# A zero-pass filler with a higher target and true job sizes, and a start with its blanking moved between engines, in a gated mix of two attention blocks

## Chip, cores, metric

The kernel runs on one core of one Trainium2 chip. The metric is device time in microseconds (us). The time is about 1.8 us more than the span from the first to the last instruction that the profile shows. A run counts as slow when it is over 1.5% above the fastest of the same kernel; only fast runs enter ratios.

## The reference, cut to what matters

```python
g = sigmoid((x * gate_w).sum(-1))          # x: 2048 x 512, bf16
a = softmax_attention(x, A_wqkv, A_wo)     # 32 heads of 16, all 2048 x 2048 scores
b = local_attention(x, B_wqkv, B_wo)       # 32 heads, 8 keys at distance 0, 2, .. 14
return g * a + (1 - g) * b
```

Block `a` needs 32 x 2048 x 2048 exponentials. They are the bulk of the work.

## The kernel before

The attention of block `a` runs in 32 periods, one for each pair of a 512-row piece of the queries and a group of four heads. In a period TensorE writes scores into two PSUM tiles (`ring`, of 1536 and of 1024 columns), ScalarE takes exponentials of them (`pT`), and TensorE multiplies those with V into the accumulator `acc`. About a tenth of the score tiles goes to a bank `w` and gets its exponential from a polynomial on VectorE (`ta`, `pd`). GpSimd does block `b`.

The order of all instructions is fixed when the kernel is built: a small event simulation, the plan, has queues, durations and priorities, and emits instructions in its own order of time. The plan also fills idle stretches of TensorE with matmuls of a zero weight, "zero passes", so that the clock gate does not halve TensorE's clock:

```python
    HAM = 3.4133                  # us, the length of one step of the clock gate
    share = 0.55                  # target: streamed share of such a step
    def idle_fill(self, st):      # st: when the next TensorE job can start
        t = self.free["pe"]
        gap = st - t - 0.18
        if self.filler is None or gap < 0.1:
            return
        lo = st - self.HAM
        ...
        have = sum(b - max(a, lo) for a, b in self.streamed)
        need = min(gap, self.share * self.HAM - have)
        if need < 0.05:
            return
        d = self.filler(need)
        if d:
            self.stream(t, d)
            self.free["pe"] = t + d
    ...
    # a job of planned duration x[4] counts as x[4] - 0.11 us of streaming:
    self.stream(st, x[4] - 0.11)
```

```python
    def fill_pass(need):
        p = acc_open[0]
        if p is None:                       # before the first accumulator: into a bank of its own
            ...
        j = max(range(4), key=lambda j_: row_left[p][j_])
        if row_left[p][j] == 0:             # accumulator complete: no pass
            return 0.0
        n = int(need * 2400.0 / 64.0) * 64
        done = 0
        while done < n:                     # adds zero to the open accumulator
            m = min(QW, n - done)
            mm(acc_tiles[p][32 * j:32 * j + 32, 0:m], z32[:], filling(m), False, False, tile_position=(0, 32 * j))
            ...
```

A zero pass lies in a planned gap and ends 0.18 us before the next job, so it moves nothing else in the plan.

At the start, the projection weights are spread from `wraw` into padded tiles `wkp` and `wqp`, whose padding must be zero. GpSimd (`G`) blanks most of it; VectorE (`V`) copies the first columns of `wqp`:

```python
    V.memset(wqp[:, :, 0:1], 0.0)
    for i0, i1 in ((0, 1), (1, NG)):
        G.memset(wkp[:, :, i0:i1], 0.0)
        G.tensor_copy(out=wkp[:, :, i0:i1, ...], in_=wraw[:, 0, :, i0 * 64:i1 * 64] ...)
        if i0 == 0:
            G.memset(wqp[:, :, 1:NG], 0.0)
    ...
    def w_job():
        yield ("delay", 8.0)
        yield ("dve", 1, 1.0, lambda: wq_part(V, 0, 1))
        yield ("set", ev_wq)
```

Of the kernel before, what the change touches and what calls it, by code (L numbers as in the profile page):

```python
# [19 lines left out]
DH = 16  # L20
# [31 lines left out]
class Plan:  # L52
# [79 lines left out]
            return  # L132

    HAM = 3.4133
    share = 0.55
    filler = None

    def stream(self, t, d):
        self.streamed.append((t, t + d))

    def idle_fill(self, st):
# [6 lines that stand above are left out]
        while self.streamed and self.streamed[0][1] < lo:  # L148
            self.streamed.popleft()
        have = sum(b - max(a, lo) for a, b in self.streamed)  # L150
        need = min(gap, self.share * self.HAM - have)
        if need < 0.05:
            return
        d = self.filler(need)
        if d:
            self.stream(t, d)
            self.free["pe"] = t + d
# [16 lines left out]
    def run(self):  # L174
        while True:
            best = None
            for e, lst in self.ready.items():
                rs = []
                for x in lst:
                    g_ = self.gate(x[6])  # L180
                    if g_ is not None:
                        rs.append(max(x[2], g_))
                if rs:
                    st = max(self.free[e], min(rs))
                    if best is None or st < best[0]:
                        best = (st, 1, e)
            for r, lst in self.reqs.items():
                if lst and self.slots[r]:
                    st = max(min(x[0] for x in self.slots[r]), min(x[2] for x in lst))
                    if best is None or st <= best[0]:  # L190
                        best = (st, 0, r)
            if best is None:
                return
            st, kind, nm = best
            self.now = st
            if kind == 0:
                lst = self.reqs[nm]
                x = min(y for y in lst if y[2] <= st + 1e-9)
                lst.remove(x)
                s = min(y for y in self.slots[nm] if y[0] <= st + 1e-9)  # L200
                self.slots[nm].remove(s)
                self.advance(x[3], st, s[1])
            else:
                lst = self.ready[nm]
                ok = [y for y in lst if y[2] <= st + 1e-9 and self.gate(y[6]) is not None
                      and self.gate(y[6]) <= st + 1e-9]
                x = min(ok, key=lambda y: (y[0], y[1]))
                if nm == "pe" and not self.fits(x, st):
                    for y in ok:
                        y[2] = max(y[2], st + 0.1)  # L210
                    continue
                lst.remove(x)
                if nm == "pe":
                    self.idle_fill(st)
                if x[6] is not None:
                    slot = self.take(x[6], st)
                    self.held["job"] += 1
                    more = x[5](slot)
                else:
                    more = x[5]()  # L220
                if isinstance(more, float):
                    x[4] += more
                if nm == "pe":
                    self.stream(st, x[4] - 0.11)
                if CFG_DEBUG:
                    LOG.append((st, x[4], nm, getattr(x[3], '__name__', '?'), x[0]))
                self.free[nm] = st + x[4]
                self.advance(x[3], st + x[4] + self.LAT[nm], None)
# [3 lines left out]
def kernel(  # L232
# [95 lines left out]
    SP.dma_start(out=awo[:], in_=A_wo.rearrange("(c p) n -> p c n", p=128))  # L328
    warm = const.tile([128, 1], BF16, name="warm")

    make_identity(nc, ident[:])
    V.memset(z32[:], 0.0)
    V.memset(warm[:], 0.0)
    A.activation(out=warm[:], in_=warm[:], func=ACT.Exp)
    heat = ps.tile([128, QW], FP32, tag="acc", bufs=1, name="heat")
    V.memset(wqp[:, :, 0:1], 0.0)
    for i0, i1 in ((0, 1), (1, NG)):
        G.memset(wkp[:, :, i0:i1], 0.0)
        G.tensor_copy(out=wkp[:, :, i0:i1, :, 0:DH].rearrange("p c i j d -> p c (i j) d"),
                      in_=wraw[:, 0, :, i0 * 64:i1 * 64].rearrange("p c (h d) -> p c h d", d=DH))  # L340
        if i0 == 0:
            G.memset(wqp[:, :, 1:NG], 0.0)
    make_identity(nc, identf[:])
    V.memset(selq[:], 0.0)
    for j in range(4):
        V.memset(selq[32 * j:32 * j + DH, 32 * j + DH:32 * j + DH + 1], 1.0)
# [3 lines left out]
    V.scalar_tensor_tensor(out=kbias[:], in0=qbias[:], scalar=256.0, in1=k16[:], op0=ALU.mult, op1=ALU.add)  # L350
    V.tensor_scalar(out=qbias[:], in0=qbias[:], scalar1=VOFF / 256.0, scalar2=None, op0=ALU.mult)

    def wq_part(eng, i0, i1):
        eng.tensor_copy(out=wqp[:, :, i0:i1, :, 0:DH].rearrange("p c i j d -> p c (i j) d"),
                        in_=wraw[:, 1, :, i0 * 64:i1 * 64].rearrange("p c (h d) -> p c h d", d=DH))
    wq_part(G, 1, NG)
    G.memset(vp_all[:, :, :, DH:DH + 1], 1.0)
    G.memset(maskb[:], 0.0)
    G.affine_select(out=maskb[:], in_=maskb[:], compare_op=ALU.is_ge, fill=NEG,
# [1 line left out]
    zpad = work.tile([128, 2 * D], BF16, name="zpad", tag="kvs", bufs=1)  # L361
    G.memset(zpad[:], 0.0)
    SP.dma_start(out=kv_scr[0:16, :], in_=zpad[0:16, :])


    P = Plan(["pe", "act", "dve", "pool", "sp"])
# [54 lines left out]
    ev_kv = [Event() for _ in range(NT)]  # L421
    ev_kdone = Event()
    ev_wq = Event()
    ev_turned = [Event() for _ in range(NC)]
    ev_final = [Event() for _ in range(NC)]
    k_left = [NG * NC]
# [4 lines left out]
    final_left = [TPC] * NC  # L431

    xts = {}
    ev_xfree = {0: Event(), 1: ev_x[1], 2: Event()}

    def x_job(sc):
        yield ("delay", XARR[sc])
# [8 lines left out]
    def x_half(sc, hf, xt, left):  # L446
        v = xt[:, hf, :].bitcast(BF16).rearrange("p (c t) -> p c t", c=DC)

        def tr():
            for tt in range(2):  # L450
                for c in range(DC):
                    PE.transpose(out=v[:, c, tt * 128:(tt + 1) * 128],
                                 in_=xr[sc // 2][:, sc % 2, 2 * hf + tt, c * 128:(c + 1) * 128], identity=ident[:])
        yield ("pe", 0, 0.70, tr)
        dst = xT[:, :, sc * QW + hf * 256:sc * QW + (hf + 1) * 256]
        if hf == 0:
            yield ("dve", 1, 0.62, lambda: V.tensor_copy(out=dst, in_=v))
        else:
            yield ("act", 0, 1.05, lambda: A.copy(out=dst, in_=v))
        left[0] -= 1  # L460
        if left[0] == 0:
            yield ("set", ev_x[sc])

    def w_job():
        yield ("delay", 8.0)
        yield ("dve", 1, 1.0, lambda: wq_part(V, 0, 1))
        yield ("set", ev_wq)

    def k_job(i, sc, rel, prio):
        if rel is not None:  # L470
            yield ("wait", rel)
        yield ("wait", ev_x[sc])
        w = Bank()
        ring = i == 0 and sc % 2 == 0

        def pe(s=None):
            if ring:
# [31 lines left out]
    def v_job(h0, h1, tb, TB, rel, prio):  # L509
# [7 lines left out]
        def pe(t0, t1):  # L517
            def f(s=None):
                if t0 == 0:
                    w.open(s, [128, TB, n])  # L520
                for tt in range(t0, t1):
                    for c in range(DC):
                        mm(w.t[:, tt, :], xT[:, c, (tb + tt) * 128:(tb + tt + 1) * 128],
                           wv[:, c, h0 * DH:h1 * DH], c == 0, c == DC - 1)
            return f
        step = TB if TB < 8 else TB // 2
        one = 4 * max(0.06, n / 2400.0)
# [12 lines left out]
    def q_job(p, rel, prio):  # L540
        c_, i = periods[p]
        if rel is not None:
            yield ("wait", rel)
        yield ("wait", ev_x[c_])
        yield ("wait", ev_wq)
        if p > 0:
            yield ("wait", ev_sel[i])
# [27 lines left out]
    def g_job(prio):  # L575
# [5 lines left out]
        def pe(t0):  # L581
            def f(s=None):
                if t0 == 0:
                    w.open(s, [128, NT])
                for t in range(t0, t0 + 4):
                    for c in range(DC):
                        mm(w.t[:, t:t + 1], xT[:, c, t * 128:(t + 1) * 128], gw[:, c:c + 1], c == 0, c == DC - 1)
            return f
# [26 lines left out]

    acc_open = [None]

    def fill_pass(need):
        p = acc_open[0]
        if p is None:  # L620
            if P.now > 30.0:
# [5 lines left out]
                njunk[0] += m  # L627
            return n / 2400.0
        j = max(range(4), key=lambda j_: row_left[p][j_])
        if row_left[p][j] == 0:  # L630
            return 0.0
        n = int(need * 2400.0 / 64.0) * 64
        done = 0
        while done < n:
            m = min(QW, n - done)
            mm(acc_tiles[p][32 * j:32 * j + 32, 0:m], z32[:], filling(m), False, False, tile_position=(0, 32 * j))
            done += m
            njunk[0] += m
# [300 lines left out]
    def ot_job(c_, cb):  # L939
# [2 lines left out]
        w = Bank()  # L942

        def tr(s):
            w.open(s, [128, QW], BF16)
            for tt in range(TPC):
                PE.transpose(out=w.t[:, tt * 128:(tt + 1) * 128], in_=otok_tiles[c_][:, tt, cb * 128:(cb + 1) * 128],
                             identity=ident[:])
# [102 lines left out]
    def b_attn(t, rel, prio):  # L1051
# [140 lines left out]
            yield ("wait", ev_final[0])  # L1192

        def fin2(s):
            w2.open(s, [128, DC, 128], BF16)
            for c in range(DC):
                PE.transpose(out=w2.t[:, c, :], in_=st["obb"][:, c * 128:(c + 1) * 128], identity=ident[:])
# [35 lines left out]
            P.spawn(v_job(h0, h1, tb, TB, rel, prio + 0.01 * tb))  # L1233

    ev_acc[0].time = 0.0
    P.free["pe"] = 1.3
    P.free["dve"] = 3.0
    P.free["act"] = 2.5
    for sc in range(NC):
        P.spawn(x_job(sc))  # L1240
    P.spawn(w_job())
# [73 lines left out]
```

## Time and profile before

| | before |
|---|---|
| median of the first three runs | 903.26 us (901.75 to 906.38) |
| span of the profiled run | 904.6 us |
| first exponential starts, last one ends | 25.5 us, 891.5 us |
| mean granted TensorE clock | 0.965 |

The page of the profile: busy time of the engines, then the busy share of ScalarE (ACT) and the granted TensorE clock (PEclk) in 40 equal slices, in tenths, 9 being 90% or more.

```profile
span 904.6 us, 15324 instructions
...
PE 765.2 (85%) x5825; PEld 263.6 (29%) x5825; DVE 786.7 (87%) x1381; ACT 846.9 (94%) x755; POOL 587.7 (65%) x546
...
ACT  2799999999999999999899999999999999999994
...
PEclk9599999999999999999899999999999999997999
...
```

ScalarE is busy 94% of the span, so it bounds the kernel, and the first slice and the last show where most of its idle time lies. The PEclk line has a 5 in the second slice: TensorE ran there at half clock.

What ScalarE waited for between 30 and 890 us (us in total, times, the longest):

```profile
...
ACT pT L277 <- PE ring L277: 9.5, 21, 1.1
ACT pT L277 <- PE w L277: 9.3, 16, 1.8
...
```

These are some 19 us, and nearly all come from TensorE being late. Seven stretches in which the granted clock fell, four of them shown, with the busy time of each engine in them and the sum of all seven (window, its length, busy time and number of instructions by engine, granted clock, DMA share, GB/s):

```profile
...
core 0: us, PE busy (x) PEld busy (x) DVE busy (x) ACT busy (x) POOL busy (x), PEclk, DMA share, GB/s
...
276.00:282.00 6.00, 5.13 (x36) 1.65 (x36) 4.30 (x9) 4.15 (x4) 4.64 (x5) 0.72 0.00 0
436.00:446.00 10.00, 9.02 (x53) 2.57 (x53) 7.06 (x14) 7.98 (x8) 9.52 (x9) 0.66 0.07 25
...
628.00:636.00 8.00, 7.14 (x42) 2.15 (x41) 4.63 (x9) 5.94 (x6) 7.84 (x8) 0.57 0.11 36
821.00:834.00 13.00, 12.22 (x72) 2.69 (x71) 10.63 (x19) 11.85 (x12) 12.53 (x12) 0.61 0.13 47
sum 55.00, PE 50.01 PEld 13.58 DVE 41.43 ACT 46.27 POOL 42.30; mean PE 7.14 PEld 1.94 DVE 5.92 ACT 6.61 POOL 6.04
```

ScalarE was busy 46.27 of these 55 us, so 8.7 us are missing there. The same view in two long stretches, from the first exponential on:

```profile
...
25.50:46.00 20.50, 20.33 (x179) 6.89 (x179) 10.19 (x18) 17.58 (x16) 0.00 (x0) 0.52 0.01 1
46.00:890.00 844.00, 718.86 (x5472) 243.20 (x5470) 755.63 (x1321) 822.34 (x733) 572.38 (x528) 0.98 0.15 48
...
```

In the first 20.5 us of exponentials the clock was 0.52, and ScalarE lost 2.9 us; in the following 844 us it lost 21.7 us.

What ended up in a half-clock stretch can be read from TensorE's timeline just before 437.7 us (start, duration, engine, instruction, number, idle time before it and what ended that):

```profile
...
434.18 0.39 PE L277 MATMUL ring<-qt,kt_all 32*128 32x512 bf16 x2
434.50 0.60 PE L277 MATMUL acc<-pT,vp_all 128*17 128x512 bf16 x5
435.44 0.39 PE L277 MATMUL ring<-qt,kt_all 32*128 32x512 bf16 x3 [0.35 <-ACT pT L277]
436.36 0.39 PE L277 MATMUL ring<-qt,kt_all 32*128 32x512 bf16 x2 [0.52 <-ACT pT L277]
...
436.68 0.39 PE L277 MATMUL acc<-pT,vp_all 128*17 128x512 bf16 x4
437.70 0.61 PE L277 MATMUL ring<-qt,kt_all 32*128 32x512 bf16 x3 [0.62 <-ACT pT L277]
```

TensorE waits three times for ScalarE, 0.62 us at the longest, and no zero pass stands in these gaps: two lie before the period's last matmuls into `acc` (436.68), the third after them, when by the code the filler had nowhere to put a pass. From 437.7 us on the same three `ring` matmuls take 0.61 us instead of 0.39: the clock is halved.

The start, 9.8 to 26 us:

```profile
...
9.89 3.17 DVE L277 COPY wqp<-wraw 128x256 bf16<-128x256 bf16 x1 [1.39 <-DMA wraw<-in_A_wqkv_dram]
...
9.90 3.08 POOL L277 MEMSET wkp<- 128x3584 bf16 x1
...
10.15 2.91 DVE L277 COPY xT<-xt 128x1024 bf16<-128x1024 bf16 x1
11.09 1.97 DVE L277 TENSOR_SCALAR kt_all<-xt,kbias 128x512 bf16<-128x512 f32 x1
...
25.53 1.45 ACT L277 ACTIVATE pT<-ring 128x1536 bf16<-128x1536 f32 x1 [6.46 <-PE ring L277]
```

VectorE's copy of 256 columns took 3.17 us. It began as GpSimd's memset began and ended as that one ended, and two instructions of VectorE stood in the queue behind it. The first exponential waited until 25.53 us.

The exponentials, the zero passes into `acc` (128 of them open an accumulator), and the weight loads of all zero passes, from the page's costliest groups (number, then busy us and mean ns, then idle time before them):

```profile
...
L277 ACT ACTIVATE pT<-ring 128x1536 bf16<-128x1536 f32 x732 | 838.8, 1290 | 30.0 <-PE ring L277 16.4
...
L277 PE MATMUL acc<-ident,z 128*32 128x512 bf16 (+6 forms) x469 | 105.0, 349 | 8.2 <-DVE accS L277 8.1
...
L277 PEld LDWEIGHTS <-z 128*32 128x32 bf16 x481 | 30.3, 95 | 57.6 <-issue 53.2
...
```

### The profile page before, as it was taken

How to read it: one execution, taken by the hardware profiler on the slowest of the kernel's cores; microseconds unless marked ns; L12 is line 12 of the kernel's file. 1: busy time of each engine (PE TensorE's matmuls, PEld its weight loads, DVE VectorE, ACT ScalarE, POOL GpSimd, SP SyncE). 2: the span in 40 equal slices, each digit the busy share in tenths (PEclk: the TensorE clock that was granted, in tenths of full speed). 3: DMA queues.
4: the chain of work that ended last, by engine and by line, in shares of the span. 5: the costliest groups of instructions: out<-in, count | busy, mean ns of one | idle time of the engine just before them, and what ended most of it. 6: DMA issues, size and time to landing. Idle time of an engine off the chain costs nothing.

```text
span 904.6 us, 15324 instructions
## 1 busy us (share of the span) xinstructions
PE 765.2 (85%) x5825; PEld 263.6 (29%) x5825; DVE 786.7 (87%) x1381; ACT 846.9 (94%) x755; POOL 587.7 (65%) x546
## 2 busy tenths in 40 slices
PE   6988898888997888888888898988888888889776
PEld 4333232223422223222222222322222222222222
DVE  5588988899898998999798988999899989888995
ACT  2799999999999999999899999999999999999994
POOL 6000636839584777868689649893949895969540
PEclk9599999999999999999899999999999999997999
DMA  8000303011012130033030120313111030201000
GB/s 280 1 2 13 93 1 106 1 59 47 1 59 64 43 95 12 2 103 105 13 106 30 39 75 12 117 47 105 47 59 48 1 117 7 99 1 47 1 2 23
DMA packets 43802, 47.15 MB, mean 52 GB/s; under 512 B 1728, under 2 KB 41152, under 8 KB 43728
## 3 DMA queue, kind: packets, MB, share of 16 engines
q1 hardware_dynamic: 42144, 45.13, 15.6%
q10 hardware_dynamic: 1584, 1.05, 0.4%
q8 instruction: 45, 0.74, 0.3%
q14 instruction: 29, 0.24, 0.1%
HBM read 39.85 MB, written 6.32 MB: 51 GB/s over the span
## 4 chain that ended last, share of the span: by engine, by line
ACT 40%; PE 27%; issue 17%; DVE 15%; DMA 1%; ACTq 0%; DVEq 0%
ACT pT L277 39%; PE w L277 11%; PE ring L277 8%; DVE ta L277 7%; PE acc L277 7%; DVE pd L277 2%; DVE kt_all L277 1%; DMA wraw<-in_A_wqkv_dram 1%; DVE kmax_all L277 1%; DVE qt L277 1%; DVE absq L277 1%; DVE accS L277 1%; ACT lg L277 1%; DVE lg L277 0%; DVE osb L277 0%
## 5 line engine op out<-in xcount | busy, mean ns | idle before, releaser
L277 ACT ACTIVATE pT<-ring 128x1536 bf16<-128x1536 f32 x732 | 838.8, 1290 | 30.0 <-PE ring L277 16.4
L277 PE MATMUL ring<-qt,kt_all 32*128 32x512 bf16 x1829 | 294.0, 393 | 108.1 <-ACT pT L277 99.6
L277 DVE SCALAR_TENSOR_TENSOR ta<-ta,w 128x512 f32<-128x512 f32 x438 | 294.8, 681 | 6.0
L277 POOL TENSOR_TENSOR prod<-vsh,lg 128x512 f32<-128x512 bf16 x128 | 136.5, 1099 | 167.3 <-issue 109.9
L277 POOL TENSOR_TENSOR prod<-prod 128x512 f32<-128x512 f32 (+1 forms) x208 | 239.9, 1167 | 6.3
L277 PE MATMUL acc<-pT,vp_all 128*17 128x512 bf16 x1829 | 233.6, 393 | 0.1
L277 POOL TENSOR_TENSOR prod<-ksh,qb 128x512 f32<-128x512 bf16 x128 | 144.1, 1158 | 99.3 <-DVE qb L277 90.4
L277 PEld LDWEIGHTS <-kt_all 32*128 32x128 bf16 x2048 | 101.5, 91 | 360.5 <-issue 347.6
L277 DVE TENSOR_SCALAR ta<-w 128x512 f32<-128x512 uint16 x219 | 150.0, 686 | 42.0 <-PE w L277 40.5
L277 DVE SCALAR_TENSOR_TENSOR pd<-ta,w 128x512 uint16<-128x512 f32 x219 | 148.6, 680 | 2.8
L277 PE MATMUL acc<-ident,z 128*32 128x512 bf16 (+6 forms) x469 | 105.0, 349 | 8.2 <-DVE accS L277 8.1
L277 PE MATMUL w<-qt,kt_all 32*128 32x512 bf16 x219 | 85.7, 394 | 0.0
L277 PE MATMUL acc<-pd,vp_all 128*17 128x512 bf16 x219 | 76.7, 395 | 0.0
L277 PEld LDWEIGHTS <-vp_all 128*17 128x17 bf16 x2048 | 44.7, 88 | 89.9 <-issue 87.6
L277 PE MATMUL w<-bw,xT 128*128 128x512 bf16 x192 | 49.9, 382 | 1.9 <-DVE qt L277 0.6
L277 PEld LDWEIGHTS <-z 128*32 128x32 bf16 x481 | 30.3, 95 | 57.6 <-issue 53.2
L277 PEld LDWEIGHTS <-xT 128*128 128x128 bf16 x512 | 32.8, 100 | 37.8 <-issue 24.5
L277 PE MATMUL w<-xT,wqp 128*128 128x512 bf16 x128 | 35.4, 401 | 3.0 <-DVE kt_all L277 2.1
L277 DVE TENSOR_SCALAR absq<-w 128x512 int16<-128x512 int16 x32 | 22.0, 688 | 14.9 <-PE w L277 14.9
L277 PE MATMUL w<-xT,wkp 128*128 128x512 bf16 x120 | 31.4, 384 | 1.1 <-DVE kt_all L277 1.0
L277 DVE CAST kvs<-w 128x512 bf16<-128x512 f32 x32 | 21.9, 685 | 7.2 <-PE w L277 6.9
L277 DVE TENSOR_SCALAR kt_all<-w,kbias 128x512 bf16<-128x512 f32 x30 | 22.4, 746 | 6.6 <-PE w L277 6.4
(80 smaller groups left out, 462.8 us busy)
## 6 DMA issues: line engine op xcount, KB each, us to landing
ksh<-kv_scr SPq DMA_DIRECT2D x16, 1024.0 KB, 7.1
vsh<-kv_scr SPq DMA_DIRECT2D x16, 1024.0 KB, 6.4
kv_scr<-kvs SPq DMA_DIRECT2D x16, 256.0 KB, 2.3
xr<-in_A_x_dram SPq DMA_DIRECT2D x4, 512.0 KB, 8.6
out_dram<-osb SPq DMA_DIRECT2D x16, 128.0 KB, 1.7
bw<-in_B_wqkv_dram SPq DMA_DIRECT2D x1, 1536.0 KB, 11.8
wraw<-in_A_wqkv_dram ACTq DMA_DIRECT2D x2, 512.0 KB, 7.1
wv<-in_A_wqkv_dram SPq DMA_DIRECT2D x1, 512.0 KB, 11.0
```

The source lines that it names most:

```text
L277: return chain_on(self._key, f(*a, **k))
```

## The change

The intent: keep the clock up by more zero passes in the right places, and start the exponentials earlier. The core of the diff:

```diff
-    share = 0.55
+    share = 0.70
+    thin = 0.0
...
-        d = self.filler(need)
+        d = self.filler(need, t)
...
-                    self.stream(st, x[4] - 0.11)
+                    self.stream(st, x[4] - 0.11 - self.thin)
+                    self.thin = 0.0
...
-    V.memset(wqp[:, :, 0:1], 0.0)
-    for i0, i1 in ((0, 1), (1, NG)):
-        G.memset(wkp[:, :, i0:i1], 0.0)
-        G.tensor_copy(out=wkp[...], in_=wraw[...])
-        if i0 == 0:
-            G.memset(wqp[:, :, 1:NG], 0.0)
+    V.memset(wkp[:].rearrange("p c i j d -> p (c i j d)").bitcast(U32), 0)
+    V.memset(wqp[:].rearrange("p c i j d -> p (c i j d)").bitcast(U32), 0)
...    (the copies of columns 1 to NG stay on GpSimd, after its small memsets)
-    ev_xfree = {0: Event(), 1: ev_x[1], 2: Event()}
+    ev_xfree = {0: ev_x[0], 1: ev_x[1], 2: Event()}
...    (P.thin is set in five kinds of jobs: transposes of x, o and b, V projections, gate;
...     it is what their planned duration holds beyond the columns that they stream)
     def w_job():
-        yield ("delay", 8.0)
-        yield ("dve", 1, 1.0, lambda: wq_part(V, 0, 1))
+        yield ("delay", 6.5)
+        yield ("act", -1, 0.45, lambda: w_part(A.copy, wkp, 0, 0, 1))
+        yield ("set", ev_wk)
+        yield ("delay", 1.5)
+        yield ("act", -1, 0.45, lambda: w_part(A.copy, wqp, 1, 0, 1))
         yield ("set", ev_wq)
...
-        ring = i == 0 and sc % 2 == 0
+        ring = i == 0 and sc == 2
...
-        yield ("wait", ev_x[c_])
+        yield ("wait", ev_x[c_ if p else 2])
...
-        if row_left[p][j] == 0:
-            return 0.0
+        if row_left[p][j] == 0:
+            if not P.free_at("w", t0 - 0.2):
+                return 0.0
+            slot = P.take("w", t0 - 0.2)
+            wt = wtile(slot, [128, QW])
+            while done < n:
+                m = min(QW, n - done)
+                mm(wt[0:32, 0:m], z32[:], filling(m), True, True, tile_position=(0, 0))
+                done += m
...
-    P.free["pe"] = 1.3
-    P.free["dve"] = 3.0
-    P.free["act"] = 2.5
+    P.free["pe"] = 1.8
+    P.free["dve"] = 4.0
+    P.free["act"] = 4.0
```

More of the change, by code (lines that the diff above doesn't have):

```diff
@@ L329 @@
     warm = const.tile([128, 1], BF16, name="warm")
+    U32 = mybir.dt.uint32
     make_identity(nc, ident[:])
@@ L335 @@
     heat = ps.tile([128, QW], FP32, tag="acc", bufs=1, name="heat")
-    V.memset(wqp[:, :, 0:1], 0.0)
-    for i0, i1 in ((0, 1), (1, NG)):
-        G.memset(wkp[:, :, i0:i1], 0.0)
-        G.tensor_copy(out=wkp[:, :, i0:i1, :, 0:DH].rearrange("p c i j d -> p c (i j) d"),
-                      in_=wraw[:, 0, :, i0 * 64:i1 * 64].rearrange("p c (h d) -> p c h d", d=DH))
-        if i0 == 0:
-            G.memset(wqp[:, :, 1:NG], 0.0)
-    make_identity(nc, identf[:])
+    V.memset(wkp[:].rearrange("p c i j d -> p (c i j d)").bitcast(U32), 0)
+    V.memset(wqp[:].rearrange("p c i j d -> p (c i j d)").bitcast(U32), 0)
     V.memset(selq[:], 0.0)
@@ L351, with w_part @@
     V.tensor_scalar(out=qbias[:], in0=qbias[:], scalar1=VOFF / 256.0, scalar2=None, op0=ALU.mult)
-    def wq_part(eng, i0, i1):
-        eng.tensor_copy(out=wqp[:, :, i0:i1, :, 0:DH].rearrange("p c i j d -> p c (i j) d"),
-                        in_=wraw[:, 1, :, i0 * 64:i1 * 64].rearrange("p c (h d) -> p c h d", d=DH))
-    wq_part(G, 1, NG)
+    def w_part(copy, dst, z, i0, i1):
+        copy(out=dst[:, :, i0:i1, :, 0:DH].rearrange("p c i j d -> p c (i j) d"),
+             in_=wraw[:, z, :, i0 * 64:i1 * 64].rearrange("p c (h d) -> p c h d", d=DH))
+    make_identity(nc, identf[:])
     G.memset(vp_all[:, :, :, DH:DH + 1], 1.0)
@@ L363 @@
     SP.dma_start(out=kv_scr[0:16, :], in_=zpad[0:16, :])
+    w_part(G.tensor_copy, wkp, 0, 1, NG)
+    w_part(G.tensor_copy, wqp, 1, 1, NG)
     P = Plan(["pe", "act", "dve", "pool", "sp"])
@@ L423 @@
     ev_wq = Event()
+    ev_wk = Event()
     ev_turned = [Event() for _ in range(NC)]
@@ L449, in tr @@
         def tr():
+            P.thin = 0.16
             for tt in range(2):
@@ L471, in k_job @@
             yield ("wait", rel)
+        yield ("wait", ev_wk)
         yield ("wait", ev_x[sc])
         w = Bank()
-        ring = i == 0 and sc % 2 == 0
+        ring = i == 0 and sc == 2
         def pe(s=None):
@@ L524, in f @@
                            wv[:, c, h0 * DH:h1 * DH], c == 0, c == DC - 1)
+                P.thin = (t1 - t0) * (one - 4 * n / 2400.0)
             return f
@@ L585, in f @@
                 for t in range(t0, t0 + 4):
+                    P.thin = 0.65
                     for c in range(DC):
@@ L616, with fill_pass @@
     acc_open = [None]
-    def fill_pass(need):
+    def fill_pass(need, t0):
         p = acc_open[0]
@@ L629, in fill_pass @@
         j = max(range(4), key=lambda j_: row_left[p][j_])
-        if row_left[p][j] == 0:
-            return 0.0
         n = int(need * 2400.0 / 64.0) * 64
         done = 0
+        if row_left[p][j] == 0:
[7 more added lines that the diff above has]
+                done += m
+            njunk[0] += n
+            P.slots["w"].append((P.now, slot))
+            return n / 2400.0
         while done < n:
@@ L944, in tr @@
         def tr(s):
+            P.thin = 0.18
             w.open(s, [128, QW], BF16)
@@ L1194, in fin2 @@
         def fin2(s):
+            P.thin = 0.18
             w2.open(s, [128, DC, 128], BF16)
```

## The prediction

> **What bounds it now.** The page's busy table: ScalarE 94% of 904.6 us (731 exponentials, 838.8 us), VectorE 87%, TensorE 85%. ScalarE's 58 us idle are: 25.5 before the first exponential, 13 after the last (timeline of both ends), about 20 between 30 and 890 us (ScalarE's waits: 9.5 on `ring` scores, 9.3 on `w` matmuls). Most of those 20 fall where the granted TensorE clock is 0.50: the table of windows shows it below 0.99 at 24-46, 154-158, 277-282, 437-446, 523-527, 560-566, 629-636 and 821-834 us, and the ScalarE time missing there is about 12 us, 3 of them in 24-46. The clock changes in steps of 3.41 us. From the matmul records I summed the columns streamed per step: the seven steady-state drops follow steps at 0.36 to 0.51 of full rate[...]. The Trainium skill, "TensorE: Matmul & The Clock Gate", Part 1, states the same window (3413 ns) and two states, but no threshold; the trace suggests 0.42.
>
> **What the change does.**
> 1. Filling target 0.55 to 0.70 of a window; five thin jobs no longer counted as full streaming; zero passes also while an accumulator is closed. Fill goes into planned gaps, ending 0.18 us before the next job, so the plan hardly moves. Before has 469 zero passes into `acc` (128 open accumulators); estimate from counts and widths: 50 us of filler. I expect twice that, TensorE 90% busy or more. Its idle time is mostly "ring waits for ScalarE" (99.6 us), so mostly free, but it was slack in which a late TensorE caught up, and a fill in a `w` bank can wait for VectorE's last read: 1 to 4 us lost.
> 2. Start. GpSimd's memsets (3.1 us each) and VectorE's copy into `wqp` collide: it took 3.18 us (9.89 to 13.06) beside GpSimd's memset (9.90 to 12.98); the second `xT` copy and `kt_all` queue behind it. The Trainium skill, "SBUF — State Buffer", describes an exclusive port lock between the two; this trace agrees. After: two memsets on VectorE, estimated from 0.272 us for 256 words and 0.112 for 64 at 1.8 us each, over before the first `xT` copy at 7.8; ScalarE copies the first columns (about 0.45 us, estimated from 1.01 for 1024). `x` chunk 2 no longer waits for the first K eviction. First exponential 3 to 5 us earlier.
>
> **Sum.** Start -4; early half-clock stretch -3; later drops, which cost 9, give back 7.5; interference +2. 903.3 - 12.5 = about 891. The tail of 13 us and the number of exponentials (731, within 5) stay.
>
> **Prediction.** 890.5 us, 8 in 10 between 883 and 899. Faster by over 2% (below 885.2) 0.20, within 2% 0.77, slower 0.03.
>
> **What would show it.** Mean granted clock 0.965 to at least 0.985; no half-clock stretch at 24-46, at most two in the steady part. First exponential at 20 to 22.5. No 3 us copy on VectorE near 10 us. ScalarE's idle from 30 to 890 us from 20 to about 10. Zero passes near 900.
>
> **What would make it wrong.** Fill eats the slack and scores come late: ScalarE's `ring` waits grow at full clock. The drops remain because plan and chip drift apart and gaps are not where the plan thinks. A ScalarE copy waiting for the second weight load holds up the `xT` copy behind it. Or a better gain, if drops also cost by shifting work later.

## The result

The changed kernel took 889.73 us (median of 4 runs, 888.66 to 893.25), against 903.94 us before (median of 4). The ratio is 0.9849, with a 95% interval of 0.9811 to 0.9887. A ratio here is the mean time of one kernel's fast runs over that of the other's of the same rounds, so it is not quite the ratio of the medians; this one lies within 2%.

The page after:

```profile
span 887.9 us, 15924 instructions
...
PE 790.9 (89%) x6125; PEld 280.7 (32%) x6125; DVE 786.3 (89%) x1381; ACT 845.5 (95%) x757; POOL 581.1 (65%) x542
...
ACT  3999999999999999999999999999999999999994
...
PEclk9899999999999999999999999999999999999999
...
```

The half-clock slice is gone and TensorE's busy share rose from 85% to 89%. ScalarE's waits between 30 and 873 us:

```profile
...
ACT pT L279 <- PE w L279: 7.5, 13, 1.7
ACT pT L279 <- PE ring L279: 2.2, 7, 0.7
...
```

The waits for `ring` scores fell from 9.5 to 2.2 us. Three lines and the sum of the same seven stretches of clock time, now without half clock but for the last:

```profile
...
276.00:282.00 6.00, 5.51 (x40) 1.65 (x39) 5.29 (x10) 5.89 (x6) 0.00 (x0) 1.00 0.06 20
436.00:446.00 10.00, 8.23 (x71) 2.90 (x65) 8.35 (x15) 9.88 (x10) 9.76 (x9) 1.00 0.01 2
...
821.00:834.00 13.00, 11.30 (x83) 4.06 (x84) 11.39 (x23) 12.58 (x13) 5.37 (x6) 0.87 0.00 1
sum 55.00, PE 49.17 PEld 16.30 DVE 49.27 ACT 54.34 POOL 38.76; mean PE 7.02 PEld 2.33 DVE 7.04 ACT 7.76 POOL 5.54
```

Of the 55 us ScalarE is busy 54.34, where it was 46.27. The stretches are the same times and not the same work, so the two sums compare what a quiet and a half-clock stretch let through. From the first exponential on:

```profile
...
21.00:41.50 20.50, 19.75 (x200) 7.26 (x200) 12.94 (x23) 19.61 (x18) 0.00 (x0) 0.83 0.01 2
41.50:873.50 832.00, 746.81 (x5748) 261.63 (x5746) 751.56 (x1317) 818.23 (x731) 572.72 (x528) 1.00 0.15 48
...
```

The start:

```profile
...
9.83 0.41 ACT L279 COPY wqp<-wraw 128x256 bf16<-128x256 bf16 x1 [0.76 <-DMA wraw<-in_A_wqkv_dram]
...
10.26 0.69 DVE L279 COPY xT<-xt 128x1024 bf16<-128x1024 bf16 x1 [2.24 <-PE xt L279]
...
11.13 0.75 DVE L279 TENSOR_SCALAR kt_all<-w,kbias 128x512 bf16<-128x512 f32 x1 [0.17 <-PE w L279]
...
21.04 5.97 ACT L279 ACTIVATE pT<-ring 128x1536 bf16<-128x1536 f32 x5 [5.11 <-PE ring L279]
...
```

The copy into `wqp` takes 0.41 us on ScalarE, VectorE's next two instructions take 0.69 and 0.75 us, and the first exponential starts at 21.04 us.

```profile
...
L279 ACT ACTIVATE pT<-ring 128x1536 bf16<-128x1536 f32 x732 | 836.7, 1300 | 19.1 <-PE w L279 7.5
...
L279 PE MATMUL acc<-ident,z 128*32 128x512 bf16 (+6 forms) x736 | 166.7, 340 | 5.5 <-DVE accS L279 5.4
...
L279 PEld LDWEIGHTS <-z 128*32 128x32 bf16 x781 | 51.6, 95 | 80.0 <-issue 63.0
...
```

There are 781 zero passes instead of 481. Without the 128 that open accumulators, and summing the widths of the rest, the filler grew from 127,000 to 251,000 columns. (In time that is 53 and 105 us, an estimate at the 2.4 GHz that the Trainium skill, "TensorE: Matmul & The Clock Gate", Part 1, gives for the full clock.)

The 16.7 us between the two profiled spans add up like this. The first exponential starts 4.5 us earlier (of which some 1.2 us come by way of the clock, see `wq_act`). In the first 20.5 us of exponentials ScalarE loses 0.9 instead of 2.9 us (2.0 us won). After that it loses 13.8 (832 - 818.23) instead of 21.7 us (7.9 won). ScalarE's own busy time in the two stretches together fell by 2.1 us (839.9 to 837.8). The tail after the last exponential is 13.1 us in both. The profiled run of before was at the slow end of its runs, so the medians differ by 14.2 us, not by 16.7.

### The profile page after: what moved, and what is told of

It reads as the page before. It is cut to its first block, busy times and chain, and to the rows that moved or that the text cites. A ratio compares the mean times of both kernels' runs of the same rounds, so it can differ in the third digit from the quotient of the medians.

```text
span 887.9 us, 15924 instructions
## 1 busy us (share of the span) xinstructions
PE 790.9 (89%) x6125; PEld 280.7 (32%) x6125; DVE 786.3 (89%) x1381; ACT 845.5 (95%) x757; POOL 581.1 (65%) x542
## 4 chain that ended last, share of the span: by engine, by line
ACT 44%; PE 23%; issue 18%; DVE 14%; DMA 1%; SPq 0%; ACTq 0%; DVEq 0%
ACT pT L279 44%; PE w L279 10%; PE ring L279 7%; DVE ta L279 7%; PE acc L279 5%; DVE pd L279 2%; DMA xr<-in_A_x_dram 1%; DVE kt_all L279 1%; DVE kmax_all L279 1%; DVE absq L279 1%; ACT lg L279 0%; DVE qt L279 0%; DVE accS L279 0%; DVE kvs L279 0%; DVE ssum L279 0%
## 5 line engine op out<-in xcount | busy, mean ns | idle before, releaser
L279 PE MATMUL ring<-qt,kt_all 32*128 32x512 bf16 x1829 | 287.7, 384 | 75.1 <-ACT pT L279 62.5
L279 PE MATMUL acc<-pT,vp_all 128*17 128x512 bf16 x1829 | 228.2, 385 | 0.0
L279 PEld LDWEIGHTS <-kt_all 32*128 32x128 bf16 x2048 | 105.1, 91 | 316.4 <-issue 300.5
L279 PE MATMUL acc<-ident,z 128*32 128x512 bf16 (+6 forms) x736 | 166.7, 340 | 5.5 <-DVE accS L279 5.4
L279 PE MATMUL w<-qt,kt_all 32*128 32x512 bf16 x219 | 83.9, 385 | 0.0
L279 PEld LDWEIGHTS <-z 128*32 128x32 bf16 x781 | 51.6, 95 | 80.0 <-issue 63.0
L279 PE MATMUL acc<-pd,vp_all 128*17 128x512 bf16 x219 | 74.7, 384 | 0.0
L279 DVE TENSOR_SCALAR absq<-w 128x512 int16<-128x512 int16 x32 | 22.0, 688 | 13.7 <-PE w L279 13.6
```

Source lines behind the costliest of these rows:

```text
L279: return chain_on(self._key, f(*a, **k))
```

## The experiments

Two theories stood at the outset. One: the start gives what the first exponential shows, and all the rest comes from time at half clock, which the filler takes away at no cost. The rival: a different start puts the plan and the chip in step, or the order of jobs changed, and that removes the waits; the filler itself gives back by its cost what it wins.

One check belongs to all of them. From the traces I compared the sequences of instructions. Between before, `fill_only` and `share70_only`, and between the changed kernel and `start_only`, `nobank`, `nothin`, `share85`, `share0` and `gfill`, VectorE's and GpSimd's sequences are identical. TensorE's are identical without the zero passes, but for some 63 records that are missing from some of the traces and one pair that stands the other way round in `share0`; on ScalarE at most two records are out of place. So these runs differ in zero passes alone; `share55` fits in with them. `gjob` is the exception: the longest sequence that its 1423 instruction records of VectorE have in common with the changed kernel's is 996 long, and only 294 stand at the same place.

Below, whatever concerns a stretch of the run (first exponential, idle time, time at half clock between the first and the last exponential) is from the one profile of each kernel; times are medians of all its runs. Between the first and the last exponential the profile of before has 57.1 us at half clock and that of the changed kernel 13.7. A "drop" is a stretch at half clock. ScalarE's idle time "at full clock" is the sum of the gaps that ended while the clock was full.

### start_only: the new start, the old filling

```diff
 (from the changed kernel)
-    share = 0.70
+    share = 0.55
-                    self.stream(st, x[4] - 0.11 - self.thin)
+                    self.stream(st, x[4] - 0.11)
-            if not P.free_at("w", t0 - 0.2):
-                return 0.0
+            return 0.0
```

> The kernel before with the new start alone (share 0.55, no thin sizes, no passes while acc is closed). Theory: the whole gain is 4.5 us at the start plus about 10 us from fewer half-clock steps after it, so this one gets the start: first exponential at 21 us, 898 to 900 us (ratio 0.994 to 0.996), steady half-clock drops remain (5 or more steps, mean clock 0.965 to 0.975). Rival (the start put plan and chip in step, and that alone removed the drops): 890 us, clock 0.99.

Measured: 902.05 us (894.21 to 909.56, one of six runs slow; 901.63 over the fast ones), ratio 0.9953 (0.9885 to 1.0022). The first exponential starts at 21.1 us; the profiled span is 899.8 us against 904.6 us, 4.8 us less. Half-clock drops remain: five after the start, and mean clock 0.966. The rival is out: the new start alone keeps the drops. The interval of the ratio holds 1, so by its time alone the start is not shown to win. The median came in 2 us above what was expected; by their mean clocks the fast runs spent 57 us at half clock, those of before 47 (below), which would account for it.

### fill_only: the new filling, the old start

```diff
 (from the kernel before)
+    the changed share, thin sizes and closed-bank passes; all of the start as before
```

> The kernel before with the new filling alone, old start. Theory: first exponential stays at 25.5 us, steady drops at most 3, clock 0.985 or more, 893 to 896 us (ratio 0.988 to 0.991). Rival: the filler costs as much as it gives, 902 to 904 us.

Measured: 896.01 us (893.72 to 899.51), ratio 0.9900 (0.9853 to 0.9947), first exponential at 26.0 us, clock 0.993 in the profile, no drop between 41 us and the last exponential. As the theory expected. ScalarE's idle time between its first and its last exponential is 14.5 us, against 24.5 us in before and 14.6 us in the changed kernel.

### share55: true sizes and closed-bank passes at the old target

```diff
-    share = 0.70
+    share = 0.55
```

> The changed kernel with the target back at 0.55, true sizes and closed-bank passes kept. If the target is what matters: drops return, 896 to 899 us, clock below 0.98. If true sizes and closed-bank passes matter: within 2 us of the changed kernel (890), clock 0.985 or more.

Measured: 896.08 us (892.75 to 897.45), ratio 0.9889, clock 0.986 in the profile and 0.980 to 0.986 in all runs. The time fits the first expectation, the clock of the profile the second, so it fell between them. With 513 zero passes, only 33 more than `start_only`, it has 20.5 us at half clock between the first and the last exponential instead of 56.9. One profile of each says little, but the mean clocks of all fast runs say the same less sharply: 57 us at half clock in `start_only`, 32 here, 16 in the changed kernel, with mean times of 901.4, 895.6 and 890.3 us. So at the low target the two small parts bring about half of the filling's gain, though the intervals of `share55` and `start_only` overlap a little; the target brings the rest.

### nobank and nothin: one small part taken away at the new target

```diff
 nobank:
-            if not P.free_at("w", t0 - 0.2):
-                return 0.0
+            return 0.0
 nothin:
-                    self.stream(st, x[4] - 0.11 - self.thin)
+                    self.stream(st, x[4] - 0.11)
```

> The changed kernel without passes in a free bank while acc is closed (28 of 781 zero passes). If closed accumulators were the cause of the drops: 3 or more drops back, 893 to 897 us. If they are a detail: within 2 us of 890.

> The changed kernel with the planned sizes of the thin jobs counted as full streaming again. share55 streamed only 5.6 us more zero columns than start_only and yet had fewer half-clock steps, so the true sizes may put the passes where they are needed. If so: 893 to 897 us and 4 or more half-clock steps more than the changed kernel. If the target of 0.70 covers it: within 2 us of the changed kernel.

Measured: `nobank` 891.51 us (891.20 to 894.69), ratio 0.9852 (0.9796 to 0.9907). `nothin` 890.80 us (889.38 to 893.88), ratio 0.9873. Both are within 2 us of the changed kernel. `nothin` has 780 zero passes, one fewer than the changed kernel: at the target of 0.70 the length of the gaps, not the count of what was streamed, decides nearly everywhere how much is filled. So the true sizes of the thin jobs, named in this document's title, do next to nothing at this target.

### share70_only: the kernel before with one number changed

```diff
-    share = 0.55
+    share = 0.70
```

> The kernel before with one number changed, the target 0.55 to 0.70; thin jobs count as full, no passes while acc is closed, old start. nothin and nobank each left the changed kernel within 2 us; if both parts are truly small, this equals fill_only: 894 to 898 us, ratio 0.987 to 0.993, about 750 zero passes, at most 21 us at half clock after the first exponential. If the two parts stand in for each other: 899 us or more, over 25 us at half clock.

Measured: 896.56 us (894.63 to 900.66), ratio 0.9930 (0.9875 to 0.9985), 753 zero passes, 10.2 us at half clock between the first and the last exponential. That equals `fill_only` (896.01 us). The one number carries the filling. With `share55` this says that the target and the small parts largely stand in for each other: the target alone brings all of the gain, the small parts alone about half.

### share85: more of it

```diff
-    share = 0.70
+    share = 0.85
```

> The changed kernel with the target at 0.85: about 170 us of zero columns instead of 132. Theory (fill is nearly free while it sits in planned gaps): 887 to 891 us, at most 2 half-clock steps after 40 us, ScalarE's idle time at full clock within 2 us of 14.2. Rival (fill eats the slack in which a late TensorE caught up): ScalarE's waits for scores at full clock grow by 5 us or more, 894 us or more.

Measured: 890.29 us (889.48 to 891.37), ratio 0.9857 (0.9829 to 0.9885). It has 820 zero passes instead of 781, so the zero columns grew by 6% where I had expected 29%: the gaps were full already. ScalarE's idle time at full clock is 13.1 us against 14.2, so these passes cost nothing clear in the profile (if each gap is split where the clock changes, it is 13.6 against 12.9). Because so few were added, this run cannot say what a much denser filling would cost.

### share0: no filling

```diff
-    share = 0.70
+    share = 0.0
```

> The changed kernel with no filling at all but the passes that open an accumulator: what the clock is worth. Theory: most steps at half clock, TensorE becomes the bound, 950 to 1050 us. If the half clock mattered little in itself (rival: the gain comes from the order of jobs): under 920 us.

Measured: 956.6 us in one run, mean clock 0.82, 341 us at half clock between the first and the last exponential, in the same order of all other instructions. What ScalarE waited for in the whole span:

```profile
...
ACT pT L279 <- PE ring L279: 45.0, 60, 5.1
ACT pT L279 <- PE w L279: 25.1, 34, 2.3
...
```

The order cannot be the cause here: taking 653 zero passes away costs 67 us, in this one run.

### gjob and gfill: filling the gate jobs

The changed kernel still has two half-clock steps at 30 to 37 us. Four gate jobs lie at 25 to 33 us, before and in them; the plan takes 0.8 us for each, the trace shows about 0.48, and the plan cannot fill a gap that it does not see.

```diff
 gjob:
-                    P.thin = 0.65
+                    P.thin = 0.39
-            yield ("pe", prio, 0.8, pe(t0)) ...
+            yield ("pe", prio, 0.5, pe(t0)) ...
 gfill:
                         mm(w.t[:, t:t + 1], xT[...], gw[:, c:c + 1], c == 0, c == DC - 1)
+                if acc_open[0] is not None:
+                    fill_pass(0.22, P.now)
```

> The changed kernel with the gate jobs planned at 0.5 us instead of 0.8 (the trace shows about 0.48), so that the plan sees the gap behind each and fills it. Should remove the half-clock steps at 30 to 37 us. Those cost ScalarE only 0.5 us of idle time in the profile, so the theory expects little: 887 to 890 us. If half-clock steps cost as much everywhere (about 0.4 us for 1 us), 3 us: 886 to 888.

> The changed kernel with one zero pass of 512 columns after each of the four gate jobs, whose planned 0.8 us hide an idle stretch from the filler; durations stay, so the order of all other instructions should stay too. gjob lost with another order; here only the clock changes. Half-clock steps at 26 to 33 us gone or fewer. Theory (those steps cost ScalarE 0.5 us of idle time): 888.5 to 890 us. If the clock alone made gjob slow: 893 or more.

Measured: `gjob` 895.28 us (894.79 to 897.73), ratio 0.9917, a miss of both expectations. Its edit did not do what it was for either: the one drop before the last exponential is again of two steps, at 28.8 to 35.6 us. Its clock is the best so far (0.996), and yet it is slower than the changed kernel. ScalarE's waits:

```profile
...
ACT pT L279 <- PE ring L279: 7.6, 20, 1.0
ACT pT L279 <- PE w L279: 5.8, 12, 0.9
...
```

It waits 7.6 us for `ring` scores, where the changed kernel waits 2.2, and 18.6 of its 19.6 us of idle time are at full clock. The shorter planned duration moved the whole order. Which part of the new order costs the 5 us stays open. `gfill` keeps the order: 890.08 us (886.18 to 891.34), ratio 0.9831 (0.9792 to 0.9869), no half clock at 26 to 40 us. So the clock was not what made `gjob` slow. `gfill` is not shown to be faster than the changed kernel; their intervals overlap. A gain of 1 or 2 us from the early steps, which is what the price worked out below would make of 6.8 us at half clock, could not be told from none here.

### wq_act and old_k: the two halves of the start

```diff
 wq_act (from the kernel before):
-        yield ("dve", 1, 1.0, lambda: wq_part(V, 0, 1))
+        yield ("act", -1, 0.45, lambda: <the same copy on ScalarE>)
 old_k (from the changed kernel):
-    ev_xfree = {0: ev_x[0], 1: ev_x[1], 2: Event()}
+    ev_xfree = {0: Event(), 1: ev_x[1], 2: Event()}
-        ring = i == 0 and sc == 2
+        ring = i == 0 and sc % 2 == 0
-        yield ("wait", ev_x[c_ if p else 2])
+        yield ("wait", ev_x[c_])
```

> The kernel before with one edit: the copy of wqp's first columns on ScalarE instead of VectorE; GpSimd's memsets stay. If the collision of VectorE's copy with GpSimd's memset is what cost the start: no 3 us copy on VectorE, second xT copy done by about 11 us, first exponential at 22 to 23.5 us instead of 25.5. If it is the new order of the K jobs: it stays at 25 to 25.5.

> The changed kernel with the K jobs, the release of the x bank and the first Q job as before; the memsets on VectorE and the copies on ScalarE stay. The other half of the start: first exponential at 22 to 23.5 us if both parts matter, 21 if only the collision did, 25 if only the K order did.

Measured, in one run each. The start of `wq_act`:

```profile
...
9.99 0.41 ACT L277 COPY wqp<-wraw 128x256 bf16<-128x256 bf16 x1 [1.11 <-DMA wraw<-in_A_wqkv_dram]
...
10.01 3.09 POOL L277 MEMSET wkp<- 128x3584 bf16 x1
...
10.25 0.69 DVE L277 COPY xT<-xt 128x1024 bf16<-128x1024 bf16 x1 [2.41 <-PE xt L277]
...
22.88 1.45 ACT L277 ACTIVATE pT<-ring 128x1536 bf16<-128x1536 f32 x1 [6.24 <-PE ring L277]
...
```

GpSimd's memset of 3.09 us is still there, ScalarE's copy beside it takes 0.41 us, VectorE's `xT` copy 0.69 us, and the first exponential comes at 22.88 us instead of 25.53. `old_k` (892.76 us in its one run):

```profile
...
22.60 2.37 ACT L279 ACTIVATE pT<-ring 128x1536 bf16<-128x1536 f32 x2 [6.24 <-PE ring L279]
```

So of the 4.5 us at the start, 2.65 go with taking VectorE's copy out of GpSimd's way (25.53 to 22.88), 1.6 with the new order of the K jobs, which project `x` to the keys (22.60 to 21.04), and 0.3 is left for the memsets on VectorE. Both parts matter, as the first expectation of each run had it.

The clock has a part in the first of these figures. The profile of before has a half-clock step at 14.4 to 17.8 us, in the middle of its start; those of `wq_act`, `old_k` and the changed kernel have none before the first exponential. `share70_only` has the start of before, collision and all, and by chance no half clock in it:

```profile
...
9.70 3.30 DVE L277 COPY wqp<-wraw 128x256 bf16<-128x256 bf16 x1 [1.90 <-DMA wraw<-in_A_wqkv_dram]
...
13.93 2.15 PE L277 MATMUL xt<-ident,xr 128*128 128x128 bf16 x32
...
24.36 2.37 ACT L277 ACTIVATE pT<-ring 128x1536 bf16<-128x1536 f32 x2 [6.24 <-PE ring L277]
```

The 32 transposes of `x` take 2.15 us here and 3.24 in before, and the first exponential comes at 24.36 us. Compared with that, moving the copy is worth 1.5 us, and the whole new start 3.3 us. The other 1.2 us of before's profile come by way of the clock: TensorE stood idle for 2.1 us behind the collision, the step in which that fell was filled 0.37 in time, and the next one ran at half clock. `fill_only`, with the same start, has such a step too and starts its exponentials at 25.97 us. All these are single profiles.

The whole time of `wq_act`, 904.9 us in a single run, shows none of this gain. By its mean clock that run spent 58 us at half clock, the fast runs of before 47 in the mean, which would hide it; but before's own runs scatter by 1 us around the line below, and its profiled run lies almost 3 us under it. One run cannot show a gain of this size.

### The runs themselves as an experiment

The steps of the clock gate are not tied to the start of the kernel: in the trace of before they begin 0.7 us after the first instruction, in that of the changed kernel 2.7 us. The same program falls into half clock for a different time in each run; that the lie of the steps is the reason is likely, but not shown. Each run's span and mean granted clock are recorded. Time at half clock is then 2 x (1 - clock) x span. A straight line of time on it, over the fast runs; the last column takes the slope of before, 0.27, for every kernel:

| kernel | fast runs | mean time at half clock, us | mean time, us | us of time for each us at half clock | own line at zero, us | at zero with 0.27, us |
|---|---|---|---|---|---|---|
| before | 35 | 47 | 904.4 | 0.27 | 891.8 | 891.7 |
| share70_only | 6 | 20 | 897.0 | 0.38 | 889.3 | 891.5 |
| fill_only | 6 | 18 | 896.6 | 0.43 | 888.9 | 891.7 |
| start_only | 5 | 57 | 901.4 | 0.29 | 885.0 | 886.1 |
| changed | 4 | 16 | 890.3 | 0.38 | 884.2 | 886.0 |
| gjob | 4 | 10 | 895.8 | 0.24 | 893.3 | 893.0 |

For before the correlation is 0.96 over half-clock times from 27 to 75 us. The last two columns are extrapolations. With few runs a kernel's own slope is rough (its standard error is 0.01 for before, 0.03 to 0.11 for the others), so the last column is the safer one, and it sorts the kernels by what is not the clock. The three with the old start come to 891.5 to 891.7 us with either filling, and `start_only` and the changed kernel to 886. The other kernels with the new start and its order (`share55`, `nobank`, `nothin`, `share85`, `gfill`) come to 885.9 to 887.5. So at equal time at half clock the filler neither wins nor costs more than about 1.5 us: what it wins it wins through the clock. Of the 14.1 us between the means of before and changed, 31 us less at half clock at 0.27 make 8.4 us; 5.7 are left for the start, which by the first exponential made 3.3 to 4.5; the rest is not explained. `gjob` stands out with 893 us: its order is the worse one whatever the clock.

The price of 0.27 holds for such small times only. `share0` has 343 us at half clock and 67 us more than the changed kernel, which makes 0.20 for each us. A line over runs is also no experiment: something else that differs from run to run could move both. The experiment is `share0`, where only the passes were taken away.

## Why the prediction was right

The predicted time, 890.5 us, was met (889.73), and the mechanism was the one predicted. That the number fits so closely is in part luck: the terms were read from the profile of a run of before at the slow end (906.4 us) and taken from the median of 903.3, so their sum was too large for the medians, and the cost of 2 us that did not come had been set against it. By terms:

- Start, -4: measured -4.5 in the first exponential, 3.3 of it without the half-clock step that before's profile happened to have there. The collision that the prediction read from two overlapping lines is shown by `wq_act`. The Trainium skill, "SBUF — State Buffer", section "Who interferes with whom", has the lock held for a whole instruction; here VectorE's copy, 3.17 us, ended 0.08 us after GpSimd's memset. (When the copy began, at 9.89 us, GpSimd's memset before that one was still running, from 6.88 to 9.97.)
- Early half-clock stretch, -3: measured -2.0. The prediction said there would be no half clock at 24 to 46 us; two steps remain at 30 to 37 us, around the gate jobs, whose planned 0.8 us hid their idle time from the filler. `gfill`, which fills behind these jobs, has no such steps and wins nothing that shows.
- Later drops, -7.5: measured -7.9, and two single steps at half clock remain in the steady part (at 214 and 825 us), as many as allowed.
- Interference, +2: not seen. ScalarE's waits for scores fell rather than grew, its idle time at full clock went from 16.6 to 14.2 us, and with one slope the old and the new filling meet at zero half clock. This term measured about zero. It was small, and the 2 us by which ScalarE's own busy time fell were not foreseen either.
- Filler doubled: yes in columns (127,000 to 251,000), but in 781 passes and not near 900, with TensorE at 89% and not 90%. Without the opening ones there are 653 passes instead of 353, and their mean width grew from 360 to 385 columns.
- The share at which the clock falls: with the steps laid at the edges of the clock's record, the seven steady drops of before follow steps at 0.37 to 0.44 of full rate (the 0.36 to 0.51 of the prediction come out with the steps laid 0.3 us earlier).
- What the prediction left in one lump, target, true sizes and closed-bank passes, can be had from the target alone: `share70_only` equals `fill_only`.

Other marks held: mean clock 0.992 (at least 0.985), ScalarE's waits from 30 us to the end of the exponentials 10.6 us ("about 10"), and the number of exponentials is the same in both (732; the prediction had miscounted by one).

## What to carry to other kernels

When a clock gate works in fixed steps, look at what was streamed in each step, not at the longest idle gap; padding planned gaps with harmless matmuls cost nothing that showed here, where another engine was the bound, and with the gaps nearly full a higher target added little. Compare runs at equal granted clock, or fit a line over the runs, before you believe a change of one per cent: the fast runs of before alone went from 898.1 to 913.4 us, in step with their time at half clock. When a schedule comes out of a simulation, change one duration and the order changes with it; test a filler by adding passes that leave all planned durations as they are.

## What the Trainium skill lacked or had wrong

- "TensorE: Matmul & The Clock Gate", "Why this matters for your kernels", advises against idle gaps of more than about 3 us, and Part 1 gives the step of 3413 ns and the two clocks but no share at which the gate closes; one of its cases has frequent short idles make the clock swing, again without a share. Here six of the seven steady drops of before followed steps whose longest gap between matmul records was 0.42 to 0.60 us (the seventh shows 1.71 us). Gaps do not tell them apart: of 227 full-clock steps between 50 and 885 us that were followed by full clock, 102 held a gap of 0.42 us or more, 15 one of 0.6 or more. The streamed share does: 0.37 to 0.44 of the full rate before the seven drops, and 0.44 or more in all but two (0.41, 0.42) of the steps that were followed by full clock. So short gaps alone do not keep the clock up. (The shares are sums of column counts from the matmul records over 2.4 columns per ns times the granted clock, simultaneous matmuls counted once.)
- For the way back the same page asks for one busy window, about 3.4 us of sustained work, and gives no share. In before, half-clock steps followed by full clock were filled 0.67 to 0.85 in time (one 0.99), those followed by another half-clock step 0.69 to 0.82. The two ranges overlap, so no threshold can be read from these records, some of which are missing.
- The same page puts the penalty at half of the time at half clock; no page prices it for a kernel that TensorE does not bound. Here it was 0.27 us of time for each us at half clock (35 fast runs of before).
- "SBUF — State Buffer", "Who interferes with whom", agrees: VectorE's copy 3.17 us beside GpSimd's memset, ScalarE's copy of the same columns 0.41 us beside one, and a VectorE copy out of PSUM 0.69 us beside one.
- "VectorE: DVE Perf Modes", "Zero memsets can be issued as uint32 (trn2)", says one cycle per element; "Trainium Kernel Development and Optimization" lists VectorE at 0.96 GHz, which makes 2.13 us for 2048 words, an estimate. The two memset records of 2048 words read 1.765 us, which is shorter; the start of the second came 2.14 us after that of the first, which agrees.
- No page of those I used says that the record of the granted clock can begin late: it begins 7.6 us after the first instruction in before and 6.1 us in the changed kernel, the profile's clock reads 1.00 until then, and in before the first nine zero passes of 512 columns took 602 ns in the mean, the later ones of that width 404 ns.
